# Retention and two MLPs on one core: the carried state as 128 rows by 64 columns, its products on 64x64 quarters of TensorE

## The chip, the cores and the metric

The kernel runs on one core of a Trainium2 chip. The time is device microseconds of one execution; 576.1 us is the median of three runs. Profiles hold one execution, with times from the start of its span.

## The reference

A retention layer (attention without softmax, computed block by block with a carried state) feeds two MLPs. The shapes are B = 2, H = 8 heads, S = 768 positions, D = 64 per head; the MLPs take 1536 tokens of width 512 to width 2048 and back, and every weight arrives as 64-bit floats.

```python
for b in range(nb):                        # blocks of positions
    intra = einsum('bhic,bhjc->bhij', qb, kb) * Dmask
    intra = einsum('bhij,bhjd->bhid', intra, vb)
    inter = einsum('bhid,bhde->bhie', qb * lam_pow, kv_state)
    out[:, :, sl] = intra + inter
    kv_state = lam_block * kv_state + einsum('bhsd,bhse->bhde', kb_dec, vb)
x = out.transpose(0, 2, 1, 3).reshape(B * S, H * D)
h = maximum(x @ w_in, 0.0);  x = h * h @ w_out          # first MLP
h = x @ w2_in;  return maximum(0.01 * h, h) @ w2_out     # second MLP
```

## The kernel before

**Units.** The retention works in 12 units: 2 batches times 6 blocks (c = 0 to 5) of 128 positions. The 8 heads are 4 head pairs p, and par = 0 or 1 is the head within its pair. A head's 64 columns lie on 64 partitions, so a pair fills 128. For one unit, TensorE transposes k and q (L294), multiplies the two to scores (L311, one PSUM bank for each par), forms the new state's addend from the decayed keys kd and v (L335), and forms the output (L360 and L362) as the sum of two products in one PSUM bank: the carried state times the scaled queries qS (only where c > 0, so in 10 of the 12 units), and v times the masked scores Pm.

**The state.** `st` is two tiles, used in turn, of 128 rows by 4 pairs by 128 columns. Each pair's 128x128 block is zero except for its two 64x64 diagonal blocks. The zeros are written once by POOL (L321). An update is done for each par by itself: POOL multiplies the old block by the decay (L342, `tmp`), and VectorE adds the PSUM addend (L347, or copies it where c = 0, L349).

**Array shapes.** The profile writes the part of TensorE that a matmul uses as rows*columns: 128*128 for transposes and the MLPs, 64*128 for scores, 128*64 for L335, L360 and L362 (two of these side by side cover the array). A float32 matmul is two instructions on the array; the MLPs' fp32r matmuls are one.

**Evacuation.** `split` copies the output bank to xhi on ScalarE (L68) and writes the rest to xlo on VectorE (L69). x is stored with head pairs as its four chunks of 128 rows; the first MLP contracts over these chunks.

**Order.** TensorE and the DMA queue of SyncE (SP) follow the program as written. In iteration i of the loop over units TensorE does the transposes of unit i + 2, the state addend of unit i, the output of unit i and the scores of unit i + 2. The order on VectorE, ScalarE and POOL is set by the scheduler when the program is built. All loads are issued by SP in one order: k, q, v of coming units, and in iterations 1 and 9 a chunk of the first MLP's weights (`fetch`, tile `raw`, 1 MB).

**Weights.** A fetched chunk is converted on the chip to two fp32r parts by `converting`: ScalarE takes the absolute value (L114) and a copy (L135), VectorE does six steps over 128x1024 elements (L115, L116, L118, L121, L122, L125) and a last one (L137). One step is taken in each of the iterations 3 to 9, and the rest beside the MLPs' matmuls. In some stages VectorE also forms sums of weight blocks (L437 to L442) and sums of activations (L449 to L451, L491) for a product scheme with seven instead of eight block products (`second_pair`).

**PSUM.** All tiles come from one pool of 8 banks; a unit takes six of them (two for transposes, one for the state, one for the output, two for scores).

**The MLPs.** All their matmuls are at L503. The first MLP is worked in four stages of 512 hidden columns, then the second in the same way.

## Time and profile before

| | |
|---|---|
| median of 3 runs | 576.1 us (575.93 to 576.34) |
| the profiled execution | 576.42 us, of which the span is 574.5 us |
| TensorE matmul busy | 564.2 us (98%) |
| VectorE, ScalarE, POOL busy | 418.4, 305.0, 83.9 us |
| granted TensorE clock | full (1.00) over the whole span |
| HBM read, written | 52.43 MB, 27.80 MB |

The span is the time from the first to the last instruction; 1.9 us of the execution lie around it. Busy time counts an engine as busy while any of its instructions is under way. Matmuls overlap, so a TensorE shown as busy can still have lost time between two starts; where that matters, starts are compared with starts.

### The profile page before, as it was taken

What the parts mean: (1) busy time and instruction counts of PE and PEld (TensorE: products, weight loads), DVE (VectorE), ACT (ScalarE), POOL (GpSimd) and SP (SyncE); (2) the same over time, 40 slices, a digit from 0 to 9 for tenths busy, and PEclk for the clock granted to TensorE, in tenths of its full rate; (3) what the DMA queues carried; (4) which work ended last, traced back from release to release, by engine and by line L of the source; (5) the groups of instructions that cost most, each with busy time, mean ns of one, the idle gap of its engine ahead of it and who ended that gap; (6) DMA issues with size and microseconds to landing.
All of it is one profiled execution on the core that took longest, in us unless ns stands there. A gap on an engine that the chain in (4) does not pass through costs nothing.

```text
span 574.5 us, 8051 instructions
## 1 busy us (share of the span) xinstructions
PE 564.2 (98%) x3075; PEld 470.7 (82%) x3075; DVE 418.4 (73%) x589; ACT 305.0 (53%) x477; POOL 83.9 (15%) x101
## 2 busy tenths in 40 slices
PE   7989999999999999999999999999999999999997
PEld 6878888888788888888888888888888888888886
DVE  3879999999927599498478999929873996217222
ACT  2344598546757687758448374553562376225110
POOL 3426000000040105445000000000203011310000
PEclk9999999999999999999999999999999999999999
DMA  8997434665492649999713216341529523661432
GB/s 172 239 213 177 156 121 138 234 183 180 172 164 57 73 148 181 203 249 189 185 36 91 76 41 216 128 165 74 103 55 246 109 29 47 76 90 56 162 113 92
DMA packets 74071, 78.12 MB, mean 136 GB/s; under 512 B 40105, under 2 KB 46513, under 8 KB 74033
## 3 DMA queue, kind: packets, MB, share of 16 engines
q1 hardware_dynamic: 60448, 60.57, 34.6%
q0 software_dynamic: 13056, 16.78, 20.9%
q8 instruction: 24, 0.39, 0.3%
q10 hardware_dynamic: 528, 0.26, 0.2%
q14 instruction: 15, 0.11, 0.1%
HBM read 52.43 MB, written 27.80 MB: 140 GB/s over the span
## 4 chain that ended last, share of the span: by engine, by line
PE 74%; DVE 15%; DMA 6%; issue 3%; SPq 1%; ACT 1%; POOL 0%; DVEq 0%; POOLq 0%; ACTq 0%
PE ps L503 72%; DMA raw<-in_moe_w_in 2%; DVE rb L122 2%; DMA raw<-in_moe_w_out 2%; DVE hb L125 2%; DVE hb L118 2%; SPq L65 1%; DVE rb L121 1%; DVE hb L115 1%; DVE Pm L316 1%; DMA k<-in_k 1%; DVE xlo L69 1%; DVE w1l L137 0%; DVE g1l L474 0%; DVE sw L442 0%
## 5 line engine op out<-in xcount | busy, mean ns | idle before, releaser
L503 PE MATMUL ps<-xhi,w1h 128*128 128x512 f32 x288 | 112.1, 389 | 0.0
L503 PE MATMUL ps<-xlo,w1h 128*128 128x512 f32 x288 | 112.0, 389 | 0.0
L503 PE MATMUL ps<-xhi,w1l 128*128 128x512 f32 x288 | 112.0, 389 | 0.0
L613 POOL DMA_DIRECT2D spill<-f x48 | 46.9, 1047 | 347.6 <-ACT f L609 347.5
L609 ACT COPY f<-ps 128x512 f32<-128x512 f32 x84 | 48.9, 586 | 74.1 <-PE ps L503 72.7
L503 PEld LDWEIGHTS ps<-xhi,w1h 128*128 128x128 f32 x288 | 54.1, 188 | 11.3 <-issue 0.2
L503 PEld LDWEIGHTS ps<-xlo,w1h 128*128 128x128 f32 x288 | 54.1, 188 | 11.3
L503 PEld LDWEIGHTS ps<-xhi,w1l 128*128 128x128 f32 x288 | 54.1, 188 | 11.2
L474 DVE TENSOR_TENSOR g0l<-f,g0h 128x512 fp32r<-128x512 f32 x52 | 35.1, 687 | 33.7 <-ACT f L470 22.1
L503 PE MATMUL ps<-w2l,g0h 128*128 128x512 f32 (+1 forms) x132 | 50.5, 383 | 0.0
L503 PE MATMUL ps<-w2h,g0l 128*128 128x512 f32 (+1 forms) x132 | 50.5, 383 | 0.0
L503 PE MATMUL ps<-w2h,g0h 128*128 128x512 f32 (+1 forms) x132 | 50.5, 383 | 0.0
L137 DVE TENSOR_TENSOR w2l<-hb,w2h 128x1024 fp32r<-128x1024 f32 x16 | 19.5, 1222 | 39.8 <-ACT w2h L135 39.8
L114 ACT ACTIVATE hb<-raw 128x1024 f32<-128x1024 f32 x32 | 36.8, 1150 | 19.2 <-DVE w2l L137 7.4
L503 PE MATMUL ps<-g0h,w2h 128*128 128x512 f32 x104 | 40.5, 389 | 0.0
L503 PE MATMUL ps<-g0l,w2h 128*128 128x512 f32 x104 | 40.5, 389 | 0.0
L503 PE MATMUL ps<-g0h,w2l 128*128 128x512 f32 x104 | 40.5, 389 | 0.0
L122 DVE SCALAR_TENSOR_TENSOR rb<-raw,rb 128x1024 f32<-128x1024 uint32 x32 | 39.1, 1221 | 0.4
L125 DVE TENSOR_TENSOR hb<-hb,rb 128x1024 f32<-128x1024 f32 x32 | 39.1, 1220 | 0.4
L118 DVE SCALAR_TENSOR_TENSOR hb<-raw,hb 128x1024 uint32<-128x1024 uint32 x32 | 39.1, 1220 | 0.3
L567 DVE TENSOR_TENSOR f<-ps,f 128x512 f32<-128x512 f32 x40 | 26.2, 684 | 9.9 <-PE ps L503 9.9
L714 DVE TENSOR_TENSOR f<-ps,f 128x512 f32<-128x512 f32 (+1 forms) x25 | 16.7, 669 | 22.9 <-PE ps L503 21.7
(141 smaller groups left out, 1139.4 us busy)
## 6 DMA issues: line engine op xcount, KB each, us to landing
raw<-in_moe_w_in SPq DMA_DIRECT2D x16, 1024.0 KB, 5.6
raw<-in_moe_w_out SPq DMA_DIRECT2D x16, 1024.0 KB, 5.0
spill<-f POOLq DMA_DIRECT2D x48, 256.0 KB, 4.8
spill<-f SPq DMA_DIRECT2D x24, 256.0 KB, 2.6
f<-spill SPq DMA_DIRECT2D x24, 256.0 KB, 2.9
k<-in_k SPq DMA_DIRECT2D x12, 256.0 KB, 4.9
q<-in_q SPq DMA_DIRECT2D x12, 256.0 KB, 5.1
v<-in_v SPq DMA_DIRECT2D x12, 256.0 KB, 4.8
```

The lines of the kernel that those rows point to most:

```text
L65: return nc.sync.dma_start(dst, src)
L114: nc.scalar.activation(hf, w_hi.bitcast(F32), AF.Abs)
L118: yield ve.scalar_tensor_tensor(out=hb, in0=w_hi, scalar=0xC0000000, in1=hb, op0=ALU.bitwise_and, op1=ALU.bitwise_or)
L122: yield ve.scalar_tensor_tensor(out=rf, in0=w_lo, scalar=2.0 ** -52, in1=rf, op0=ALU.mult, op1=ALU.mult)
L125: yield ve.tensor_tensor(out=hf, in0=hf, in1=rf, op=ALU.add)
L137: yield ve.tensor_tensor(out=lo, in0=hf, in1=hi, op=ALU.subtract)
L474: nc.vector.tensor_tensor(out=glo, in0=r, in1=ghi, op=ALU.subtract)
L503: nc.tensor.matmul(ps, a, b, start=start and n == 0, stop=stop and n == len(ops) - 1, skip_group_check=again)
L567: ve.tensor_tensor(out=out, in0=ps[h, where], in1=other, op=ALU.add)
L609: nc.scalar.copy(f, src)
L613: nc.gpsimd.dma_start(dst, f, accum_op=ALU.add)
L714: nc.vector.tensor_tensor(out=a, in0=ps, in1=a, op=ALU.add)
```

## The change

The state tiles become 128 rows by 4 pairs by 64 columns, without zeros: pair p's two heads stand below each other. The zeroing is gone, and an update is one POOL and one VectorE instruction over 128 rows in place of two over 64. In `output` each state product takes 64 rows and 64 columns of the array (64*64 in place of 128*64), and it can be any of the four quarters: for even pairs head par goes from rows half par to columns half par, for odd pairs to the other half. The eight state products of a unit now stand together, ahead of the eight of L362. The output takes two banks, one for even and one for odd pairs, so that `split` runs twice on half the elements. In x the two heads of an odd pair have changed places; the rows of the first MLP's first weight matrix are therefore fetched with the halves of odd chunks exchanged, by three DMAs in place of one (eight fetches, `raw` with l = 0 and n = 0).

```diff
+    half = [slice(e * D, (e + 1) * D) for e in range(2)]
...
-            dma(r.rearrange("p (k f) -> p k f", k=k), source(*key))
+            dst, src = r.rearrange("p (k f) -> p k f", k=k), source(*key)
+            if key[0] or key[2]:
+                dma(dst, src)
+            else:
+                dma(dst[:, 0:k:2], src[:, 0:k:2])
+                for a, b in ((half[0], half[1]), (half[1], half[0])):
+                    dma(dst[a, 1:k:2], src[b, 1:k:2])
...
-            st.append(att.tile([P, NP, P], F32, name=f"st{e}"))
-            nc.gpsimd.memset(st[e], 0.0)
+            st.append(att.tile([P, NP, D], F32, name=f"st{e}"))
...
-                for par in range(2):
-                    r = slice(par * D, (par + 1) * D)
-                    nc.gpsimd.tensor_tensor(out=tmp[r], in0=old[r, :, r],
-                                            in1=LR[r, :, C - 1:C].to_broadcast([D, NP, D]), op=ALU.mult)
-            for par in range(2):
-                r = slice(par * D, (par + 1) * D)
-                if c:
-                    nc.vector.tensor_tensor(out=new[r, :, r], in0=ps[r], in1=tmp[r], op=ALU.add)
-                else:
-                    nc.vector.tensor_copy(new[r, :, r], ps[r])
+                nc.gpsimd.tensor_tensor(out=tmp, in0=old, in1=LR[:, :, C - 1:C].to_broadcast([P, NP, D]), op=ALU.mult)
+                nc.vector.tensor_tensor(out=new, in0=ps, in1=tmp, op=ALU.add)
+            else:
+                nc.vector.tensor_copy(new, ps)
...
-            ps = bank().rearrange("p (a s) -> p a s", a=NP)
-            for p in range(NP):
-
-                rows = [slice(par * D, (par + 1) * D) for par in range(2)]
-                if c:
-                    for r in rows:
-                        nc.tensor.matmul(ps[r, p, :], st[c % 2][:, p, r], qS[n][:, p, :], start=True, stop=False)
-                for par, r in enumerate(rows):
-                    nc.tensor.matmul(ps[r, p, :], vn[:, 2 * p + par, :], Pm[n][:, par, p, :], start=c == 0, stop=True)
+            ps = [bank()[:, 0:2 * C].rearrange("p (a s) -> p a s", a=2) for _ in range(2)]
+            heads = [(p, par) for p in range(NP) for par in range(2)]
+
+            def place(p, par):
+                return ps[p % 2][half[par ^ p % 2], p // 2, :]
+
+            if c:
+                for p, par in heads:
+                    nc.tensor.matmul(place(p, par), st[c % 2][half[par], p, :], qS[n][half[par], p, :],
+                                     start=p < 2, stop=False, skip_group_check=True)
+            for p, par in heads:
+                nc.tensor.matmul(place(p, par), vn[:, 2 * p + par, :], Pm[n][:, par, p, :],
+                                 start=c == 0, stop=True, skip_group_check=True)
...
-            split(xhi[t][:, :, o:o + C], xlo[t][:, :, o:o + C], ps)
+            for e in range(2):
+                split(xhi[t][:, e::2, o:o + C], xlo[t][:, e::2, o:o + C], ps[e])
```

The scheduler also places some instructions of VectorE and ScalarE elsewhere. On ScalarE the place is the first conversion step (tile `hb`, L114 before and L123 after the change), in iteration 3 of the unit loop; kT and qT are the evacuated transposes of unit 5. First before, then after:

```order
L298 COPY kT<-ps 128x512
L298 COPY qT<-ps 128x512
L68 CAST xhi_278<-ps 128x4x128
L114 ACTIVATE hb<-raw 128x1024
L298 COPY kT<-ps 128x512
L298 COPY qT<-ps 128x512
L68 CAST xhi_278<-ps 128x4x128
```

```order
L307 COPY kT<-ps 128x512
L307 COPY qT<-ps 128x512
L68 CAST xhi_276<-ps 128x2x128 x2
L307 COPY kT<-ps 128x512
L307 COPY qT<-ps 128x512
L123 ACTIVATE hb<-raw 128x1024
L68 CAST xhi_276<-ps 128x2x128 x2
```

The conversion step that needs `raw` stood ahead of the two copies of that iteration and now stands behind them.

On VectorE the same iteration has the second conversion step (L115, after the change L124); st is the state, qS the scaled queries of unit 5. First before, then after:

```order
L316 TENSOR_TENSOR Pm<-ps,DTr 128x512 x2
L115 TENSOR_SCALAR hb<-hb 128x1024
L347 TENSOR_TENSOR st_168<-ps,tmp 64x4x64
L304 TENSOR_TENSOR qS<-ps,LR 128x512
L347 TENSOR_TENSOR st_168<-ps,tmp 64x4x64
L69 TENSOR_TENSOR xlo_279<-ps,xhi_278 128x4x128
```

```order
L325 TENSOR_TENSOR Pm<-ps,DTr 128x512 x2
L349 TENSOR_TENSOR st_168<-ps,tmp 128x256
L313 TENSOR_TENSOR qS<-ps,LR 128x512
L124 TENSOR_SCALAR hb<-hb 128x1024
L69 TENSOR_TENSOR xlo_277<-ps,xhi_276 128x2x128 x2
```

The state and the scaled queries moved ahead of the conversion step.

The third place is on VectorE too, in the second stage of the first MLP, ahead of the fourth `g1l` that `activate_for_seven` writes by `split` (L69), which is the last input of a product of `second_pair`. First before, then after:

```order
L488 TENSOR_TENSOR g0l<-f,g0h 128x512
L125 TENSOR_TENSOR hb<-hb,rb 128x1024
L491 TENSOR_TENSOR f<-f 128x512
L437 TENSOR_TENSOR rb<-hb 128x256
L438 TENSOR_TENSOR rb<-hb 128x256
L439 TENSOR_TENSOR rb<-rb,hb 128x256
L440 TENSOR_TENSOR rb<-hb,rb 128x256
L69 TENSOR_TENSOR g1l<-f,g1h 128x512
```

```order
L495 TENSOR_TENSOR g0l<-f,g0h 128x512
L127 SCALAR_TENSOR_TENSOR hb<-raw,hb 128x1024
L498 TENSOR_TENSOR f<-f 128x512
L130 TENSOR_SCALAR rb<-hb 128x1024
L131 SCALAR_TENSOR_TENSOR rb<-raw,rb 128x1024
L69 TENSOR_TENSOR g1l<-f,g1h 128x512
L134 TENSOR_TENSOR hb<-hb,rb 128x1024
L456 TENSOR_TENSOR f<-f 128x512
```

One conversion step over 1024 elements (L125, after the change L134) and the four weight sums over 256 moved from ahead of this `g1l` to behind it.

## Rows read from the trace of the kernel before

**Rows 1.** Chain that ended last, 125 to 575 us: start, us, what.
```profile
148.04 0.60 DVE g0l L488
149.84 1.14 DVE rb L122
153.32 0.34 DVE rb L437
...
155.44 174.61 PE ps L503 x769
...
329.83 241.34 PE ps L503 x1076
```

**Rows 2.** Busy time by stretch, each engine: retention, stage one and start of two, rest.
```profile
20.00:63.95 43.95, 42.16 (x674) 37.63 (x672) 37.73 (x62) 18.09 (x30) 16.47 (x20) 1.00 0.94 221
63.95:155.40 91.45, 90.96 (x401) 75.00 (x400) 89.18 (x113) 64.45 (x95) 0.00 (x0) 1.00 0.48 161
155.40:571.20 415.80, 415.70 (x1844) 344.53 (x1844) 280.59 (x379) 216.07 (x342) 59.27 (x64) 1.00 0.53 120
```

**Rows 3.** Timeline of one unit: start, us, engine, instruction, count.
```profile
23.04 0.66 PE L294 MATMUL ps<-ident,k 128*128 128x128 f32 x4
23.29 1.28 DVE L316 TENSOR_TENSOR Pm<-ps,DTr 128x512 f32<-128x512 f32 x2
...
24.06 0.69 PE L335 MATMUL ps<-v,kd 128*64 128x64 f32 x16
...
24.57 0.39 PE L360 MATMUL ps<-qS,st 128*64 128x128 f32 x4
...
24.80 0.39 PE L362 MATMUL ps<-Pm,v 128*64 128x128 f32 x4
...
26.11 0.39 PE L362 MATMUL ps<-Pm,v 128*64 128x128 f32 x4
...
26.42 1.16 PE L311 MATMUL ps<-qT,kT 64*128 64x128 f32 x16
...
27.52 0.66 PE L294 MATMUL ps<-ident,k 128*128 128x128 f32 x4
```

**Rows 4.** Groups by form: busy us, mean ns, idle before.
```profile
L347 DVE TENSOR_TENSOR st<-ps,tmp 64x256 f32<-64x256 f32 x16 | 6.7, 418 | 0.5 <-PE ps L335 0.3
...
L437 DVE TENSOR_TENSOR rb<-hb 128x256 f32<-128x256 f32 x1 | 0.4, 418 | 0.0
```

**Rows 5.** Timeline around the first conversion step.
```profile
22.76 1.13 SPq L65 DMA_DIRECT2D raw<-in_moe_w_in  x1
...
24.59 1.47 SPq L65 DMA_DIRECT2D q<-in_q  x1
...
30.60 1.12 ACT L114 ACTIVATE hb<-raw 128x1024 f32<-128x1024 f32 x1 [3.47 <-DMA raw<-in_moe_w_in]
...
31.53 1.04 POOL L329 TENSOR_TENSOR kd<-k,kdec 128x512 f32<-128x512 f32 x1 [4.32 <-DMA k<-in_k]
...
32.73 0.71 PE L311 MATMUL ps<-qT,kT 64*128 64x128 f32 x8 [1.76 <-ACT qT L298]
```

**Rows 6.** Tile q, 0 to 70 us: its loads from issue to landing.
```profile
DMA to landing us min/median/max: 4.0/5.1/7.7
```

**Rows 7.** Timeline of TensorE, outputs of the last two units.
```profile
61.63 0.76 PE L360 MATMUL ps<-qS,st 128*64 128x128 f32 x3
62.07 0.32 PE L362 MATMUL ps<-Pm,v 128*64 128x128 f32 x1
62.22 0.27 PE L360 MATMUL ps<-qS,st 128*64 128x128 f32 x1
```

**Rows 8.** Timeline, second stage of the first MLP.
```profile
154.30 0.61 PE L503 MATMUL ps<-g1h,sw 128*128 128x512 f32 x2
...
154.70 0.69 DVE L69 TENSOR_TENSOR g1l<-f,g1h 128x512 fp32r<-128x512 f32 x1
...
155.44 0.50 PE L503 MATMUL ps<-g1l,sw 128*128 128x512 f32 x1 [0.53 <-DVE g1l L69]
```

## The prediction

> **What bounds the kernel now.** I read the chain that ended last from its end backwards. From 155.44 us on it is nothing but MLP matmuls, in two pieces of 174.61 and 241.34 us [rows 1]; after 155.4 us TensorE is busy 415.70 of 415.80 us [rows 2]. What happens there can't be hurried by this change, which leaves the MLP matmuls alone: the end of the kernel is the time at which TensorE comes to this stretch, plus a constant. Ahead of it there are two more. In the retention (20 to 63.95 us) TensorE is busy 42.16 of 43.95 us, and in the stretch from 63.95 to 155.4 us 90.96 of 91.45, while VectorE with 89.18 us has hardly any room either [rows 2]. So time can come from four places: shorter TensorE work in each unit, the lost 1.8 us of the retention, small losses between starts, and the wait in which the third stretch begins.
>
> The reader should see each of them. A unit's period is 27.52 - 23.04 = 4.48 us [rows 3]. The one large stall is at 32.73: the scores wait 1.76 us for the copy of q, and that copy stands on ScalarE behind a conversion step that has waited 3.47 us for its weights [rows 5]. At 62 us the fourth state instruction of the last unit comes late (below) [rows 7]. At 155.44 a matmul waits for VectorE's g1l: its start is 1.14 us after the one at 154.30, where 0.23 is the pace (174.61/769) [rows 1, 8].
>
> **TensorE in a unit.** The sixteen state instructions and sixteen of L362 start in groups of four; from the first L360 group to the last L362 group are 26.11 - 24.57 = 1.54 us for seven steps, 0.22 us a group [rows 3]. Four instructions are two matmuls, so two halves of the array work at once and a round (one instruction on each half) takes 0.11 us. The state products take 8 rounds, 0.88 us. On four quarters they would take 4, 0.44 us: -0.44 a unit.
>
> Against it stand changes of array shape. Now a unit has three: L362 to L311, L311 to L294, L294 to L335. Sixteen score instructions (two at a time) are 0.88 us, eight transposes one at a time 0.88, L335 at half the columns 0.44, L360 and L362 1.76: 3.96 of the 4.48 us. The remaining 0.52 is 0.175 for each change, and the rows have them where the shape changes: L362's last group to L311 takes 0.31 rather than 0.22, L311's sixteen 1.10 rather than 0.88 [rows 3]. L335 and L360 have one shape today; after the change there are two more changes, into 64*64 and out of it: +0.35. The unit without a state addend ahead of its output (c = 5 of the first batch) gets one. Together 9 x (-0.44 + 0.35) + (-0.44 + 0.175) = -1.0 us over the ten units with c > 0. No row shows 64*64. Its bounds: changes that cost nothing (they are free now between L335 and L360) give -4.4; two quarters at once give +3.3; one at a time +12. I take -1.0, because column halves and row halves (L311) each run side by side at full rate here, and the quarters only join the two.
>
> **The stall at 32 us.** By the new order the two copies of unit 5 stand ahead of the conversion step on ScalarE. Then its scores need no weights, and the 1.76 us are free. Next is data: TensorE would come to unit 6's transposes at 27.52 + 4.40 = 31.9 us, and to its q at 32.4. POOL's instruction that waited for that k started at 31.53 [rows 5]; q was issued at 24.59 and took at most 7.7 us, so it is there by 32.3 [rows 5, 6]. Both just arrive. Ahead of them in SP's queue the fetch is three issues for one of 1.13 us. Two more cost nothing if the transfers are the limit (the DMA share is 0.94 over this stretch [rows 2]) and 2.3 us if every issue takes 1.13, of which only what lies behind 31.9 and 32.4 counts. I take 0.1: -1.7 us; bounds -1.8 and 0. What is late next is the conversion itself, which stays at the landing of raw, 30.6. On VectorE behind it are xlo and the masks, first needed by the scores one unit later, over 3 us on. The other seven fetches have three issues as well; the second comes at the retention's end, the rest where TensorE is the bound, and I cost them nothing: 2.3 us at the second if that cover is gone.
>
> **VectorE, ScalarE, POOL.** Cost goes by columns, not rows: 64x256 and 128x256 both take 418 ns [rows 4]. In a row, 256 elements occupy VectorE for 0.34 us, 512 for 0.60, 1024 for 1.14 [rows 1]. An update saves 0.34, a split into two costs 2 x 0.34 - 0.60 = +0.08. From the conversion step at 31.75 to the g1l at 154.70 the order after has 8 such state instructions less (-2.7), 9 splits more (+0.7), the scaled queries moved ahead (-0.6), and the 1024-element step and four sums behind g1l instead of ahead (-2.5): -5.1 us.
> ScalarE's split adds less than one copy a unit (0 to 0.59 us); it is busy 18 of 44 us in the retention, POOL, with one of two updates gone, 16.5 [rows 2]: nothing on the path.
>
> **The small losses.** At 61.63 three L360 instructions start, then L362 at 62.07 and the fourth L360 only at 62.22, since the second state half is written later. L362 would have started 0.22 after 61.63. One update for both halves, ready earlier: -0.2 us, bounds -0.4 and 0.
>
> At 155 us TensorE arrives 2.9 us earlier (1.0 + 1.7 + 0.2), where it used to lose 1.14 - 0.23 = 0.9. VectorE's g1l then must be 3.8 us earlier than its end at 155.39 for no wait; it has 5.1 us less ahead of it. So -0.9 us, if the order is gone through as it stands; 0 or +0.3 if the moved steps return ahead of g1l.
>
> **PSUM.** A unit takes seven banks rather than six, so with eight the second score bank of one unit is the first of the unit before, free when VectorE has masked it. The mask at 23.29 is done with its first half at 23.93; the scores that would need its bank begin at 26.42 [rows 3]. 2.5 us of room: no cost.
>
> **Sum.** -1.0 - 1.7 - 0.2 - 0.9 = -3.8 us. The profiled execution took 576.42, which gives 572.6; it was 0.3 above the median, so against the median it is 572.3. I say 572.4.
>
> **Rivals.** (a) Two quarters at a time. The two instructions of one matmul are for the same quarter; if starts go strictly in program order, each matmul's second instruction holds up the next matmul, and a round is one matmul: 8 rounds, no gain, +3.3 for the shape changes. Against: at 62.07 an L362 instruction started ahead of an L360 instruction that stands before it and goes to the other half [rows 7]. 576.4 - 1.7 + 3.3 - 0.2 - 0.9 = 576.9, 576.6 against the median.
> The Trainium skill, "TensorE: Matmul & The Clock Gate", Part 3, says that matmuls start and end in program order, without reordering; that is this rival, and the start at 62.07 disagrees. The Trainium skill, "TensorEngine Tiling (Array Packing)", Restrictions and Gotchas, adds that different row tiles can't use one PSUM bank at the same time; here both heads of an even pair, from two row halves, write one bank (in different rows of it), which would also leave two at a time. No run here shows this.
> (b) Slower: quarters one at a time. Sixteen instructions at 0.11 are 1.76 us, 0.88 more, with the changes +1.23 a unit: +12, in all 576.4 + 12 - 2.8 = 585.6. It decides at this place alone: with -2.8 from the rest, the kernel is over 0.2% (1.15 us) slower once the state products with both changes take over 0.88 + 0.40 = 1.28 us. For it: no row has quarters; against: halves of both kinds run side by side.
> (c) The waits come back. k and q of unit 6 arrive 1.5 us late behind the three-part fetch, and g1l waits for VectorE as before (0.9 and 0.3 more): -3.8 + 2.7 = -1.1, 575.0 against the median.
> (d) Shape changes beside 128*64 cost nothing: TensorE gains 3.4 more, of which VectorE at 155 us lets through about half: 571 to 570.5.
>
> **How the numbers follow.** Forecast 0.57 (own range 571.2 to 573.8), (a) 0.13, (b) 0.06, (c) 0.15, (d) 0.09. Within 0.2% of 576.1 is 574.95 to 577.25, about what a measurement of this kernel can tell from no change. Faster: 0.57 + 0.09 + half of (c) = 0.73. Same: the other half of (c) and most of (a), 0.18. Slower: (b) and the rest of (a), 0.09. The range 570.8 to 576.9 leaves out (b), and parts of (d), (a) and the forecast, about 0.2.
>
> **What would show it.** Right: eight state instructions of a unit at 64*64 in two groups, 0.11 us from round to round with four starts in each, and two new gaps of some 0.2 us around them; units of 4.3 to 4.4 us; no wait of TensorE for the copy of q at 32 us; MLP matmuls from about 61.0 rather than 63.95; no wait for g1l near 152. Wrong: rounds of two or one; TensorE waiting for k, q or the mask; a stretch of MLP matmuls that has gaps where VectorE's moved steps are now needed.

## The result, and the profile after

| | before | after |
|---|---|---|
| median of 15 runs each on one chip | 576.34 us (575.57 to 580.11) | 581.9 us (577.39 to 585.53) |
| ratio | | 1.0086 (95%: 1.0065 to 1.0106) |
| the profiled execution | 576.42 us, span 574.5 | 577.39 us, span 575.6 |

Slower by 0.9%, where 572.4 was forecast, and outside the range. The profiled execution after is the fastest of its 15 runs. It has 1.0 us of the loss; the other 4.5 us up to the median must be looked for in another run (the first experiment).

The retention stage does what was said of it. The timeline of a unit in the kernel after, TensorE (start, time, line, shape, count), beside [rows 3]:

```profile
23.95 0.69 PE L343 MATMUL ps<-v,kd 128*64 128x64 f32 x16
24.56 0.67 PE L364 MATMUL ps<-qS,st 64*64 64x128 f32 x16
25.16 1.09 PE L367 MATMUL ps<-Pm,v 128*64 128x128 f32 x16
26.18 1.16 PE L320 MATMUL ps<-qT,kT 64*128 64x128 f32 x16
...
28.91 0.55 PE L364 MATMUL ps<-qS,st 64*64 64x128 f32 x11
```

L364 is the state product. Its sixteen instructions take 25.16 - 24.56 = 0.60 us to the next shape (forecast 0.44 and a change of 0.175), and L367's take 1.02 (0.88 and a change). A narrow window, 24.61 to 24.62 us, holds the first round alone:

```profile
24.56 0.34 PE L364 MATMUL ps<-qS,st 64*64 64x128 f32 x4
```

Four instructions have started by then, one for each quarter. The unit is 28.91 - 24.56 = 4.35 us long (forecast 4.39, before 4.48). So four quarters do work at once, and a change of shape costs about what the rows of before gave for it.

The data come later, though. TensorE and SP around 22 to 35 us, beside [rows 5]:

```profile
32.51 0.63 PE L303 MATMUL ps<-ident,k 128*128 128x128 f32 x4 [0.82 <-DMA k<-in_k]
33.61 0.63 PE L303 MATMUL ps<-ident,q 128*128 128x128 f32 x4 [0.47 <-DMA q<-in_q]
35.06 0.45 PE L343 MATMUL ps<-v,kd 128*64 128x64 f32 x8 [0.82 <-DMA v<-in_v]
```

```profile
22.35 2.49 SPq L65 DMA_DIRECT2D raw<-in_moe_w_in  x3
24.93 1.38 SPq L65 DMA_DIRECT2D k<-in_k  x1
```

The wait for the copy of q (1.76 us) is gone, as forecast; three waits for loads behind the three-part fetch, 2.11 us together, stand in its place. The first MLP matmul starts at 62.65 us, 1.3 ahead of before; forecast was 61.0.

From there on even that is lost. The windows of the kernel after, cut as in [rows 2] (length, then busy time of TensorE, weight loads, VectorE, ScalarE, POOL; granted clock, DMA share, GB/s):

```profile
20.00:63.95 43.95, 41.84 (x681) 34.65 (x680) 34.66 (x63) 19.70 (x43) 11.88 (x13) 1.00 1.01 220
63.95:155.40 91.45, 90.54 (x400) 74.66 (x399) 88.47 (x110) 64.14 (x96) 0.00 (x0) 1.00 0.48 151
155.40:571.20 415.80, 414.12 (x1836) 343.03 (x1835) 281.86 (x383) 215.48 (x341) 58.92 (x64) 1.00 0.53 122
```

The third stretch, busy 415.70 us before, now has 1.7 us without a matmul. From the first to the last start of an MLP matmul it takes 571.91 - 62.65 = 509.26 us after, 506.92 before: 2.34 lost, 1.30 gained, 1.04 slower. Two waits make it up (TensorE, then ScalarE at the second):

```profile
154.52 0.50 PE L510 MATMUL ps<-g1l,sw 128*128 128x512 f32 x1 [0.91 <-DVE g1l L69]
...
224.95 0.50 PE L510 MATMUL ps<-g1h,sw 128*128 128x512 f32 x1 [1.68 <-ACT f L616]
```

```profile
224.31 1.08 ACT L616 COPY f<-ps 128x512 f32<-128x512 f32 x2 [3.13 <-DMA partial0P<-f]
```

The first is the wait of [rows 8], still there (0.91 for 0.53). The second is new: ScalarE must copy a bank out, it has to wait for an `f` buffer, and the transfer that frees it (partial0P) takes 7.0 us to land, 5.0 before, beside a weight fetch issued 0.4 us behind it (before, 1.4 us ahead of it). That fetch is a chunk of the second weight matrix, which is still one transfer.

VectorE's stream shows why the first wait stayed:

```profile
63.25 0.69 DVE L124 TENSOR_SCALAR hb<-hb 128x1024 f32<-128x1024 f32 x1 [1.16 <-ACT hb L123]
...
117.28 0.69 DVE L124 TENSOR_SCALAR hb<-hb 128x1024 f32<-128x1024 f32 x1 [0.98 <-ACT hb L123]
...
151.31 0.69 DVE L498 TENSOR_TENSOR f<-f 128x512 f32<-128x512 f32 x1
151.91 0.69 DVE L130 TENSOR_SCALAR rb<-hb 128x1024 uint32<-128x1024 uint32 x1
152.64 1.23 DVE L131 SCALAR_TENSOR_TENSOR rb<-raw,rb 128x1024 f32<-128x1024 uint32 x1
153.78 0.69 DVE L69 TENSOR_TENSOR g1l<-f,g1h 128x512 fp32r<-128x512 f32 x1
```

L124 is the first VectorE step of a conversion; it waits for ScalarE's L123, which waits for `raw`. At 62 and 116 us VectorE stands still for weights that have not landed, 2.1 us between 60 and 155 us (0.6 before). The chunk at 62 us came in three parts; the one at 116 us is of the second matrix, in one transfer that took 6.5 us to land (4.9 before):

```profile
116.12 1.13 ACT L123 ACTIVATE hb<-raw 128x1024 f32<-128x1024 f32 x1 [2.74 <-DMA raw<-in_moe_w_out]
```

So g1l starts at 153.78, 0.9 earlier than before, where 3.8 were needed. The windows from the first VectorE step of the first conversion to this g1l, before and after, say how (the third busy time is VectorE's):

```profile
31.75:154.70 122.95, 121.94 (x896) 102.86 (x896) 119.76 (x162) 77.86 (x118) 13.24 (x15) 1.00 0.58 173
```

```profile
32.66:153.78 121.12, 119.66 (x880) 98.80 (x879) 114.31 (x157) 76.75 (x124) 8.96 (x9) 1.00 0.61 169
```

VectorE has 5.45 us less to do, as the prediction counted (5.1). But it stands still for 6.81 us in place of 3.19 and begins 0.91 later: -5.45 + 3.62 + 0.91 = -0.92.

### The profile page after: what moved, and what is told of

Read it like the earlier page. It is cut to its first block, busy times and chain, and to the rows that moved or that the text cites. A ratio compares the mean times of both kernels' runs of the same rounds, so it can differ in the third digit from the quotient of the medians.

```text
span 575.6 us, 8079 instructions
## 1 busy us (share of the span) xinstructions
PE 564.0 (98%) x3075; PEld 467.8 (81%) x3075; DVE 415.2 (72%) x591; ACT 305.6 (53%) x489; POOL 77.1 (13%) x91
## 4 chain that ended last, share of the span: by engine, by line
PE 74%; DVE 10%; issue 6%; DMA 6%; ACT 3%; POOL 0%; SPq 0%; DVEq 0%; ACTq 0%; POOLq 0%
PE ps L510 67%; DMA raw<-in_moe_w_out 2%; DVE rb L131 2%; DVE hb L127 2%; PE ps L303 2%; PE ps L367 2%; PE ps L320 1%; DMA v<-in_v 1%; DVE hb L134 1%; DMA partial0P<-f 1%; DMA raw<-in_moe_w_in 1%; DVE hb L124 1%; ACT hb L123 1%; DVE w2l L146 1%; DVE rb L130 1%
## 5 line engine op out<-in xcount | busy, mean ns | idle before, releaser
L616 ACT COPY f<-ps 128x512 f32<-128x512 f32 x84 | 48.4, 587 | 72.9 <-PE ps L510 69.6
L123 ACT ACTIVATE hb<-raw 128x1024 f32<-128x1024 f32 x32 | 36.8, 1149 | 23.8 <-DMA raw<-in_moe_w_in 9.0
L134 DVE TENSOR_TENSOR hb<-hb,rb 128x1024 f32<-128x1024 f32 x32 | 39.1, 1222 | 0.4
```

The lines of the kernel that those rows point to most:

```text
L123: nc.scalar.activation(hf, w_hi.bitcast(F32), AF.Abs)
L134: yield ve.tensor_tensor(out=hf, in0=hf, in1=rf, op=ALU.add)
L616: nc.scalar.copy(f, src)
```

## The experiments

Theory at first: the three-part fetch is what costs (F). Rivals: the waits, or the quarter products, pull the clock down (C); the new order on VectorE and ScalarE costs (S). Later, theory R: up to 157 us the end is set by VectorE, and VectorE by the landing of `raw`. All columns behind the ratio are of one profiled execution, whose time stands first and can lie far from the median (after, e3, e16). "Start" is the first MLP matmul, "raw" VectorE's waits at the first conversion step from 60 to 155 us, "150s" TensorE's waits from 145 to 165 us, "220s" its wait at 222 to 232 us, "low" the time at a granted clock of 0.50 after 20 us. Ratios are to the kernel before on the same chip (576.0 to 576.65).

An edit of the fetches also moves the order in which the scheduler places work on VectorE and ScalarE, so most pairs of runs differ in both. Two pairs do not: e17 has the order of the kernel before, and e4 that of e2, on TensorE, VectorE, ScalarE and POOL, from the first instruction to the last.

| run | median | ratio (95%) | profiled | start | raw | 150s | 220s | low |
|---|---|---|---|---|---|---|---|---|
| before | 576.3 |  | 576.42 | 63.95 | 0.6 | 0.5 | 0 | 0 |
| after | 581.90 | 1.0065 to 1.0106 | 577.39 | 62.65 | 2.1 | 0.9 | 1.7 | 0 |
| e1 after again | 580.51 | 1.0038 to 1.0085 | 580.87 | 62.39 | 4.5 | 2.9 | 1.8 | 3.4 |
| e2 one transfer | 579.46 | 1.0026 to 1.0078 | 581.99 | 61.36 | 4.8 | 5.3 | 0 | 6.8 |
| e3 before, three parts | 582.38 | 1.0081 to 1.0124 | 579.36 | 63.67 | 3.6 | 1.3 | 1.7 | 0 |
| e4 no exchange | 578.96 | 1.0028 to 1.0062 | 579.01 | 64.95 | 2.8 | 1.9 | 0 | 0 |
| e5 early fetch | 580.89 | 1.0057 to 1.0096 | 577.81 | 62.73 | 2.2 | 1.2 | 1.4 | 0 |
| e6 ahead | 584.03 | 1.0116 to 1.0157 | 584.59 | 69.41 | 2.2 | 1.1 | 1.6 | 6.8 |
| e7 filler at 153 us | 578.81 | 1.0027 to 1.0068 | 578.48 | 62.76 | 3.6 | 0.2 | 1.3 | 0 |
| e8 before, ahead | 577.16 | 1.0009 to 1.0027 | 576.75 | 63.74 | 2.4 | 0.9 | 0 | 0 |
| e9 after, no fetches | 576.80 | 1.0000 to 1.0024 | 578.59 | 67.23 | 0.3 | 0 | 0 | 6.8 |
| e10 before, no fetches | 579.53 | 1.0036 to 1.0064 | 579.53 | 67.89 | 0.3 | 0 | 0 | 0 |
| e11 gain burnt | 580.61 | 1.0043 to 1.0088 | 582.58 | 65.47 | 2.8 | 1.1 | 2.1 | 3.4 |
| e12 rows put right in x | 581.58 | 1.0050 to 1.0093 | 584.28 | 66.03 | 1.8 | 2.6 | 0 | 3.4 |
| e13 reorder | 582.68 | 1.0107 to 1.0133 | 582.29 | 62.25 | 3.1 | 3.2 | 1.6 | 6.8 |
| e14 before, reorder | 576.57 | 1.0001 to 1.0019 | 576.29 | 62.61 | 1.1 | 1.6 | 0 | 0 |
| e15 both reorders | 584.27 | 1.0104 to 1.0165 |  |  |  |  |  |  |
| e16 one transfer, reorder | 578.73 | 1.0028 to 1.0068 | 576.00 | 61.47 | 1.1 | 2.5 | 0 | 0 |
| e17 before, three of 128 | 581.05 | 1.0054 to 1.0112 | 581.22 | 64.05 | 2.8 | 3.2 | 0 | 3.4 |
| e18 before, two of 64 | 578.71 | 1.0028 to 1.0055 | 578.15 | 65.46 | 1.0 | 0 | 0.7 | 0 |

**e1.** The changed kernel word for word.

> The changed kernel once more, for a second trace of it. Theory F (the fetch in three parts delays the loads behind it and puts the weights in the way of other transfers): about 578 to 583 us, waits for k, q and v near 32 us again, and further waits that end in a DMA. Rival C (TensorE's granted clock falls in the changed retention, by the new quarter products or by the waits): the same time, but with a stretch at 0.5 that this trace shows away from the first 20 us.

Slower again, and this time the profiled execution (580.87) is near the median. VectorE and TensorE in it:

```profile
63.98 0.69 DVE L124 TENSOR_SCALAR hb<-hb 128x1024 f32<-128x1024 f32 x1 [2.15 <-ACT hb L123]
...
119.29 0.69 DVE L124 TENSOR_SCALAR hb<-hb 128x1024 f32<-128x1024 f32 x1 [2.39 <-ACT hb L123]
```

```profile
154.70 0.50 PE L510 MATMUL ps<-g1h,sw 128*128 128x512 f32 x1 [1.58 <-ACT g1h L68]
156.51 0.80 PE L510 MATMUL ps<-g1l,sw 128*128 128x512 f32 x1 [1.31 <-DVE g1l L69]
```

and its windows:

```profile
152.73:156.03 3.30, 0.90 (x3) 0.19 (x1) 3.27 (x5) 1.94 (x4) 0.00 (x0) 1.00 0.00 0
156.03:159.44 3.41, 2.92 (x7) 2.35 (x8) 3.41 (x6) 2.37 (x5) 0.76 (x1) 0.50 0.60 190
159.44:226.20 66.76, 66.76 (x296) 55.29 (x295) 45.80 (x64) 45.98 (x73) 12.40 (x15) 1.00 0.57 122
```

The same program waits 2.4 us longer for `raw` than in the first profile, TensorE stands still 2 us longer, and behind this the granted clock is 0.50 (the 1.2 GHz level) for 3.41 us: 7 matmuls where 15 fit, 1.8 us. With that the loss of this execution against the profile of before, 580.87 - 576.42 = 4.45 us, is accounted for: -1.56 (start), +2.4 (150s), +1.8 (clock), +1.8 (220s), together 4.4. Over the 24 runs of the changed kernel, the 8 with a mean clock of 0.997 or more took 577.0 to 579.7 us, the 16 with 0.994 or less 580.4 to 585.5. In the kernel before, run beside the experiments, 28 of 111 runs had a mean clock under 0.996 and no loss (median 576.29, the others 576.14). A low clock in the start-up, as in the profile of e3 (0.50 from 12.3 to 19.1 us), costs next to nothing: its MLPs started at 63.67.

**e2, e3, e4.** e2 is the changed kernel with one transfer for each chunk, e3 the kernel before with the fetch in three parts. In both, x and the rows of the first weight matrix then stand in different orders: the work is the same, the sums are not the layer's. e4 is the changed kernel with odd pairs placed like even ones (two quarters) and one transfer. The edit of e2:

```diff
-            if key[0] or key[2]:
-                dma(dst, src)
-            else:
-                dma(dst[:, 0:k:2], src[:, 0:k:2])
-                for a, b in ((half[0], half[1]), (half[1], half[0])):
-                    dma(dst[a, 1:k:2], src[b, 1:k:2])
+            dma(dst, src)
```

> The changed kernel with each chunk fetched by one DMA again; the rows of odd chunks of the first weight matrix are then not exchanged, so the product uses them in the old order. Theory F: 572 to 574 us, retention's end near 61 us, k of unit 6 at about 31.5, little spread between runs. Rival C, and a rival S (the new order on VectorE and ScalarE): 578 us or more with the same spread.

> The kernel before with the three-part fetch alone; the rows of odd chunks of the first weight matrix are exchanged although x is not. Theory F: 578 to 582 us with the spread of the changed kernel. Rivals C and S: 576 to 577 us, as before.

> The changed kernel with one DMA for a chunk and with odd pairs placed like even ones: the state products use two of the four quarters, and x keeps its order. Theory F: 3 to 4 us more than with four quarters, that is 576 to 577. Rival C by quarter products: near the changed kernel, 578 to 582. Rival C by waits: as theory F.

e3, just above theory F's range, shows that the fetch, with the order that the scheduler makes for it, makes the kernel before 1.0% slower. Its list of waits of TensorE from 145 to 232 us has the wait of the 220s, which the profiles with pieces of 64 partitions in every fetch of the first matrix have and no other:

```profile
PE ps L511 <- ACT f L617: 1.7, 1, 1.7
PE ps L511 <- DVE g1l L69: 1.3, 1, 1.3
```

e2 starts the MLPs at 61.36, near the forecast 61.0, so the three parts cost 1.3 us there. But F is not all (it had 572 to 574): e2 is still 0.5% slower, and loses it in the 150s:

```profile
PE ps L505 <- ACT g1h L68: 2.5, 1, 2.5
PE ps L505 <- DVE g0l L490: 1.9, 1, 1.9
PE ps L505 <- DVE g1l L69: 0.9, 1, 0.9
```

```profile
157.53:164.35 6.82, 6.08 (x14) 4.78 (x15) 5.30 (x9) 4.11 (x8) 1.89 (x2) 0.50 0.61 165
```

Again a low clock behind it (14 matmuls in 6.82 us, 3.6 lost). Its VectorE waits 3.0 us for one chunk, issued at 117.4 and converted from 126.6:

```profile
127.77 0.69 DVE L119 TENSOR_SCALAR hb<-hb 128x1024 f32<-128x1024 f32 x1 [3.00 <-ACT hb L118]
```

The order differs as well: in e2 and e4 the conversion step over 1024 elements and the four sums stand ahead of the g1l at 154 us again, as in the kernel before.

e4 missed theory F's 576 to 577. It shows something else. With two quarters TensorE is slower in each unit, and the first MLP matmul comes 3.59 us later than in e2 (64.95 for 61.36; F had 3 to 4 us for it). But with the same order of instructions on every engine VectorE reaches its g1l at the same time, in e2 and then in e4:

```profile
157.53 0.68 DVE L69 TENSOR_TENSOR g1l<-f,g1h 128x512 fp32r<-128x512 f32 x1
```

```profile
157.41 0.68 DVE L69 TENSOR_TENSOR g1l<-f,g1h 128x512 fp32r<-128x512 f32 x1
```

and the median is no later (578.96 for 579.46). In these executions the 3.6 us that the four quarters win for TensorE are gone at this g1l. They need not be: the three fastest of e2's twelve runs took 575.3 to 575.9 us, the fastest of e4's seven 577.6.

**e5 to e8.** e5 fetches the second chunk at unit 7 (`if i in (1, 7)`), e6 at unit 6 and with a conversion step in each of the last two units (`3 <= i <= 11`); e8 is e6's edit in the kernel before. e7 puts nine products nobody reads ahead of the ones that wait at 153 us:

```diff
+        if s == 1:
+            fill(9)
         for p in both:
             keep(product(p, "C", "S1", "T1"), kept(p, 1, 1), False)
```

> The changed kernel with one number edited: the second weight chunk is fetched two units earlier in the retention loop (at unit 7 instead of 9), when its raw buffer has long been free. Theory R (the stretch up to 157 us is set by VectorE, and VectorE's place there by when the raw words arrive: it idles from about 62 to 63.3 or 64 us for the second chunk): that idle time goes, VectorE comes 1.2 to 2.1 us earlier, the wait for g1l at 153 us shrinks to under 0.5 us, the granted clock does not fall behind it, and the median is 575.5 to 577.5. Rival C (the clock falls because of the quarter products in the retention stage, or for some other reason than the waits): the waits get shorter but the median stays at 580 or more with a mean clock of 0.99. Rival T (TensorE has to wait for something else just behind it, so that an earlier VectorE brings nothing): the median stays at 579 to 581 with new waits between 153 and 160 us.

> The changed kernel with the second weight chunk fetched at unit 6 instead of 9 and one step of conversion put into each of the last two units of the retention stage as well. Theory R (VectorE's place at 153 us is what counts, and it has idle time in the retention stage): two steps (about 1.9 us) leave the MLP stretch on top of what the early fetch brings, no wait of over 0.4 us at 149 to 158 us, median 574.5 to 576.5, that is as fast as the kernel before or faster. Rival C (clock from the products themselves): 580. Rival T: the wait is handed on, 578 to 580.

> The changed kernel with nine extra products of 128x512 (2.0 us) in TensorE's order just ahead of the products that wait at 153 us, into a bank that nobody reads. Theory R with the clock behind the waits (the wait at 153 us is real, and the low granted clock at 156 us follows from TensorE's standing still there): the nine products fill the wait and are nearly free, the granted clock stays at 1.0 behind it, the runs draw together, and the median falls from 580.5 to 577.5 to 579. Rival C (the clock falls for another reason): the clock still falls at 156 us and the nine products cost up to 2 us: 581 to 583.

> The kernel before with the second chunk fetched at unit 6 and one conversion step in each of the last two retention units, nothing else. Theory R: the kernel before has a wait of 0.9 us for g1l at 154 us and VectorE is busy from 64 us on; steps put into the retention stage take that wait away and it gains 0.5 to 1.2 us: 575.0 to 575.6. Rival T: no change within 0.3 us, 575.9 to 576.4. If the steps are in the way of the retention stage itself (they would end a unit later), it is slower by 0.5 to 2 us.

e5 is a miss: the wait at 62 us went, as R said, but VectorE gave the lead back (waits for `raw` at 114 and 139 us), TensorE waited 1.2 us in the 150s, and nothing was gained. e6 and e8 are misses too: in e6 TensorE waited 3.0 us for a k that was loaded behind the early fetch, and was clocked at 0.50 behind that (start 69.41); e8 lost 0.9 us, what it expected if the steps are in the way. e7 agrees with R and the clock behind the wait: nine products, 2.0 us, ran inside the wait (0.2 left), and the clock stayed at 1.0 there. Its median lies 1.7 us below that of e1, on another chip, and the ranges of the two ratios overlap; that the added work costs nothing can be said, that it gains can't.

**e9, e10.** No weight fetches but the first; every conversion reads that chunk again.

```diff
+            if only:
+                fetched.append((key, only[0]))
+                return
             r = raw.tile([P, 4 * CW], I64, tag="raw", name="raw")
+            only.append(r)
```

> The changed kernel without its weight fetches: only the first chunk is fetched (in three parts, as before), and every later conversion reads that chunk's raw words again, so all weights are the first chunk's. Conversions, products, spills and everything else stay. Theory R (the gain of the retention stage is real, and is lost because VectorE waits for raw words on the way to 153 us): the MLP stretch takes 507 us or less from a start at 61 to 62.5 us, no wait of over 0.5 us at 149 to 160 us, granted clock 1.0; 571 to 574 us, and 2 to 3 us below the kernel before with the same left out. Rival O (the order of VectorE's work is at fault, not the data): the wait at 153 us stays over 1 us, the granted clock falls behind it in many of the runs, and the time is 577 to 580, at or above the twin.

> The twin: the kernel before, fetching the first chunk alone and converting it again and again. In the kernel before VectorE waits for raw words hardly at all (0.3 us between 64 and 155 us), so by theory R little is gained: 574.5 to 576, which leaves it 2 to 3 us above the changed kernel's twin. Rival O: 575 to 576, and the changed kernel's twin is no faster.

The MLP stretch of e9, and one row of e10:

```profile
67.23:155.00 87.77, 87.77 (x388) 72.70 (x388) 84.48 (x111) 61.15 (x91) 0.00 (x0) 1.00 0.10 37
155.00:225.00 70.00, 70.00 (x311) 57.97 (x310) 48.91 (x66) 50.68 (x81) 13.81 (x16) 1.00 0.44 75
...
```

```profile
67.89:155.00 87.11, 87.11 (x385) 72.14 (x385) 84.18 (x108) 61.40 (x90) 0.00 (x0) 1.00 0.10 37
```

Without fetches TensorE does not miss a beat from the first to the last MLP matmul, 506.1 us in both, and the changed kernel is 2.7 us the faster of the two. Theory R had the difference and missed the rest: both start late (67.2 and 67.9, not 61 to 62.5), and both times lie above their ranges. With words always there the scheduler puts more conversion steps into the retention, in e10 with waits of TensorE for VectorE's state. So this pair changes the order as well as the data. The profiled execution of e9 (578.59) lies above its median; it has three waits for k, q and v around 33 to 36 us, 3.4 us together, and a low clock beside them:

```profile
35.06:41.89 6.83, 5.85 (x64) 5.05 (x64) 5.95 (x11) 1.79 (x5) 1.04 (x1) 0.50 1.09 215
```

That the difference comes so near the 2.9 us forecast for the retention is luck in part: the forecast took 1.7 of them from the wait for the copy of q, which is 0.6 us in e10, and had k, q and v in time, which they are not in e9.

**e11, e12.** e11 burns the gain: nine products nobody reads, ahead of the first MLP product. e12 has one transfer and puts the rows right in x, by two copies of 64 partitions for odd pairs.

> The changed kernel with nine extra products of 128x512 (2.04 us at full clock) ahead of the first MLP product, into a bank that nobody reads: they burn the gain of the retention stage on TensorE. The scheduler orders VectorE's work anew behind them. Theory R with the clock behind the waits (TensorE's earlier arrival is not what the time hangs on, and standing still at 153 us costs the clock as well): the wait at 153 us gets shorter by about as much as was burnt (under 0.4 us left), the granted clock stays at 1.0 in most runs, and the median is 577.5 to 579.5, below the changed kernel's 580.5 to 581.9 in spite of the added work. Rival C (the clock falls for another reason): the burnt time is added, 582 to 584.

> The changed kernel with every chunk fetched in one transfer and the rows put right on the other side: the output of odd head pairs is copied and split in two pieces of 64 partitions, each written to the other half of x (two more ScalarE and two more VectorE instructions per unit), so that the weights keep their order. By theory R the retention stage still ends near 61 to 62 us, VectorE waits less for raw words than the changed kernel (under 3 us between 60 and 155 us in place of 4.1), and the median is 576.5 to 579. If the extra instructions of a unit are in the way (VectorE late for the masks), the MLP starts at 63 to 64 us and the time is 578 to 580. If the order of VectorE's work counts and not the fetch, it stays at 579 to 581, as with one transfer and the weights left in their order.

In e11 TensorE came 2.8 us later to the MLPs than in the changed kernel, and the median is that of e1 (580.61 for 580.51). It was not below it, as I had expected: 1.1 us of waits were left in the 150s where under 0.4 was expected, and a wait of 2.1 us in the 220s had a low clock behind it. But the later start cost nothing, as in e4. e12 is a miss: it starts at 66.03 (waits for copies of q and for the state, 4.2 us), ends above all its ranges and tells nothing on the fetch.

**e13 to e16.** TensorE's order at 153 us, so that g1l has 2.7 us more (e13, in the kernel before e14, with one transfer e16); e15 also moves S4 behind S2 at 223 us.

```diff
-        for p in both:
-            keep(product(p, "C", "S1", "T1"), kept(p, 1, 1), False)
-            yield True
-        late_split("T3", "T1", lambda h: (1, 2 * h))
         for p in both:
             keep(product(p, "A", "A12", "B21", False), kept(p, 0, 0), False)
             yield True
         late_split("T4", "B21", lambda h: (0, 2 * h + 1))
+        if s == 1:
+            yield from c_products()
```

> The changed kernel with one edit in TensorE's order: in the second stage (around 153 us) the four groups that read g1 for the first time (C, S1 with T1) stand behind the four that read g0 (A, A12 with B21) and no longer ahead of them, so that the late g1l has 2.7 us more. VectorE's order up to there is the same. Theory W (what the changed kernel loses at 149 to 158 us is the standing still of TensorE there, and the low clock behind it): no gap over 0.5 us between 149 and 160 us, no low clock behind it, the wait of about 2 us at 223 us stays; median 577.5 to 579 (after 580.5 to 581.9). Rival V (VectorE's stream is late and sets all that follows): the gap moves to a later product of the same stage (157 to 165 us) with the same length, median 580 to 582.

> The kernel before with the same edit in TensorE's order. Theory W: its wait of 0.9 us at 154 us goes, 575.2 to 575.8. Rival V: no change, 576.0 to 576.6.

> The changed kernel with that edit, and in the third stage (around 223 us) the groups that add to bank C (S4 with B22) put behind the two that follow them (S2 with T2), so that ScalarE's copy of C, which stands still for an f buffer whose transfer to memory is late, has 2.7 us more. Theory W (both waits are all that is left): both gaps gone, MLP stretch 506.5 to 507.5 us from a start at 62.5 us, median 574.5 to 576.5, level with the kernel before or below. Rival V: the second gap stays or moves, 578 to 581.

> The changed kernel with every chunk fetched in one transfer (the rows of the first weight matrix are then not exchanged to match x) and the first of the two edits of order. With one transfer the start was at 61.4 us and the loss lay in gaps of 6 us together at 149 to 158 us, and none at 223 us. Theory W: gaps of 3 us or less are covered, two thirds of the loss goes: 575 to 577 (579.5 without the edit). Rival V: 579 to 580.

Rival V held in e13 (a little above its range) and e14; e15 came out above both ranges, e16 between them. In e13 the wait was handed on and grew (TensorE, VectorE and ScalarE):

```profile
155.55 0.80 PE L510 MATMUL ps<-g0h,w2h 128*128 128x512 f32 x1 [3.25 <-ACT f L616]
```

```profile
151.86 0.68 DVE L498 TENSOR_TENSOR f<-f 128x512 f32<-128x512 f32 x1
```

```profile
152.58 0.62 ACT L68 CAST g1h<-f 128x512 fp32r<-128x512 f32 x1 [1.35 <-DVE f L498]
...
154.93 1.05 ACT L616 COPY f<-ps 128x512 f32<-128x512 f32 x2
```

A12 adds to the bank that ScalarE must first copy out (L616), and this copy stands on ScalarE behind g1h, which waits for VectorE's L498. So this product, too, waits for VectorE. The profile of e15 is of an execution of 1459.5 us and is not read; its other runs give no gain.

**e17, e18.** The kernel before with three transfers of the changed kernel's sizes over all 128 partitions (e17), and with one transfer for each half of the partitions (e18).

```diff
                 dma(dst[:, 0:k:2], src[:, 0:k:2])
-                for a, b in ((half[0], half[1]), (half[1], half[0])):
-                    dma(dst[a, 1:k:2], src[b, 1:k:2])
+                for j in range(1, k, 2):
+                    dma(dst[:, j:j + 1], src[:, j:j + 1])
```

> The kernel before, whose chunks of the first weight matrix are fetched in three transfers of the same sizes as in the changed kernel (512, 256 and 256 KB), but each over all 128 partitions. Theory H (transfers into 64 partitions are what is slow: the chunk's 2 KB packets take 126 to 130 ns in the three-part form and 90 to 100 ns in one piece): the packets take 90 to 105 ns, no wait of 2 us at 224 us, 576.0 to 578, well below the 582.4 of the three parts with pieces of 64 partitions. Theory N (three issues in place of one, and the order that the scheduler makes for them, are what is slow): as with the pieces of 64, 580 to 583, and the gap of 2 us at 224 us.

> The kernel before, whose chunks of the first weight matrix are fetched in two transfers of 512 KB, one for each half of the partitions. Theory H: all packets go to 64 partitions at a time, so as slow as the three-part form or slower, packets of 120 ns and more, 580 to 584. Theory N: one issue more than before only, 576.5 to 579.

The window from 58 to 60 us, in which the second chunk comes in, of the kernel before, e3 and e17 (the last number is GB/s):

```profile
58.00:60.00 2.00, 2.00 (x44) 1.71 (x39) 1.94 (x5) 0.59 (x1) 0.99 (x2) 1.00 1.09 419
```

```profile
58.00:60.00 2.00, 2.00 (x42) 1.88 (x42) 1.94 (x5) 0.59 (x1) 1.24 (x2) 1.00 1.00 217
```

```profile
58.00:60.00 2.00, 2.00 (x42) 1.71 (x40) 1.94 (x5) 0.58 (x1) 0.90 (x2) 1.00 0.99 319
```

With pieces of 64 partitions the DMA engines are as busy (1.00) and bring half as much as one transfer, and two thirds of what three transfers over all partitions bring. The Trainium skill, "SBUF — State Buffer", Door 1: The DMA port swizzle, says that partitions 0 to 63, or 64 to 127, reach only half of SBUF's sixteen DMA ports; 217 GB/s beside 319 and 419 agrees in direction. The window shows the contrast at its largest: from 56 to 62 us the means are 358 (before), 268 (e3) and 315 (e17). So theory H is right that these transfers are slower.

It is wrong on the time: e17 loses 0.8% all the same, and e3's 1.0% can't be told from it. e18 ends in theory N's range. And e17 settles more than that. VectorE, ScalarE, POOL and TensorE have the instructions of the kernel before, in the same order, from the first to the last; only SP has sixteen issues more. Up to the same g1l VectorE is as long busy as before (119.81 for 119.76 us), but it stands still 2.9 us more (6.10 for 3.19), and g1l comes at 157.77, 3.1 us later:

```profile
31.86:157.77 125.91, 123.34 (x914) 103.54 (x909) 119.81 (x162) 77.22 (x118) 12.91 (x15) 1.00 0.57 167
```

```profile
157.09 0.50 PE L511 MATMUL ps<-g1h,sw 128*128 128x512 f32 x1 [2.31 <-ACT g1h L68]
158.51 0.50 PE L511 MATMUL ps<-g1l,sw 128*128 128x512 f32 x1 [0.92 <-DVE g1l L69]
```

No change of order on these engines has a part in this; the weights that land later do it. Of the 2.9 us, 2.2 are waits for `raw` after 60 us.

The wait of the 220s goes with pieces of 64 partitions, and e17 has none. But the fetch that runs beside the store there is never such a piece. In every run that has the wait, the store takes 6.6 to 7.0 us to land and a whole chunk of the second matrix is issued 0.4 us behind it; in the runs that fetch and do not wait there, 4.9 to 5.2 us, with that chunk 1.4 us ahead. So what costs there is the order of the issues, and that has moved in each of the runs with pieces and in no other.

## Why the prediction was wrong

**Held.** The quarters (0.60 us for the state products, unit 4.35 us): rivals (a) and (b) are refuted, though both heads of an even pair write one bank from two row halves. The shape changes (0.175 each): rival (d) too. The wait for the copy of q at 32 us is gone. With one transfer the MLPs start at 61.36 and 61.47 (e2, e16) for the forecast 61.0. The count of VectorE's work held as well: 5.1 us less forecast, 5.45 measured.

One reading that spoke against rival (a) was too strong. At 62.07 an L362 instruction does start ahead of the second instruction of an L360 product. But the first instruction of that product had started just before:

```profile
62.06 0.32 PE L360 MATMUL ps<-qS,st 128*64 128x128 f32 x1
```

So the products began in their order there, and only the two instructions of neighbouring ones are interleaved. Against the rival that was enough.

**Failed, a size: the fetch at 32 us.** "I take 0.1: -1.7 us; bounds -1.8 and 0." The three issues took 2.49 us, k, q and v came late by 2.11 us together, and the start is 1.3 us later than with one transfer: -0.4 in place of -1.7, near the other bound.

**Failed, the step that decides: "the other seven fetches have three issues as well ... and I cost them nothing".** They ran beside a stretch that I had read as TensorE's. It is VectorE's as much, and VectorE's pace is that of the loop in which a raw buffer is freed, fetched, landed and converted. In the kernel before this loop just closes (VectorE waits 0.6 us for it between 60 and 155 us). After, it waits 2.1 us in the first profile and 4.5 in that of e1, for whole chunks of the second matrix as well as for split ones. Three transfers for one, with the order on the four engines held, make g1l 3.1 us late and the kernel before 0.8% slower (e17). With pieces of 64 partitions it is 1.0% (e3), as much as the whole change, and the wait in the 220s comes on top, 1.7 us.

**Failed with it: "VectorE's g1l ... has 5.1 us less ahead of it".** The count stands; the place does not follow from it, since VectorE does not run through. It stood still 3.62 us more than before in one profile and 6.26 in the other, so that g1l came 0.9 us earlier in the first and 1.1 later in the second (155.78):

```profile
32.18:155.78 123.60, 120.67 (x894) 99.57 (x890) 114.15 (x158) 76.12 (x124) 8.08 (x9) 1.00 0.59 166
```

The -0.9 for that wait was +0.4 in the profiled run and +2.4 in e1.

**Failed, the frame: "the end of the kernel is the time at which TensorE comes to this stretch, plus a constant".** TensorE may come 3.6 us later at no cost to the median, with the same order on every engine (e4 beside e2). A TensorE that is early stands still in the 150s, and then the clock can take 1.8 to 3.6 us more. Rival (c), "the waits come back", was the right mechanism at the wrong price: it had no term for the clock, none for the 220s, and g1l at 0.9 + 0.3.

**Open.** e2, e4 and e16 show 0.45 to 0.5% of loss without the three parts. Waits for `raw` and the order of VectorE and ScalarE both differ from before there, with a conversion step and four sums back ahead of g1l, and no run parts the two. Nor is it shown why the landing of the same transfers differs so much from run to run, or why some waits of TensorE have a low clock behind them and others none.

No version beat the kernel before. Of those that compute the layer, e14, which is the kernel before with one edit, came nearest to it (within 0.2%).

## What to carry to other kernels

When an engine looks 98% bound, ask what its neighbour at 97% waits for: if the neighbour lives off a loop of two buffers, a gain upstream turns into a wait at the point where the two meet. Less work ahead of an instruction does not make it earlier by as much: add up busy time and idle time apart. Cost a transfer that is split or moved in every place where it runs, not only where it is first seen. And look for a run whose order of instructions is that of its twin: one such pair (e17 beside before, e4 beside e2) says more than several in which the scheduler has moved things as well.

## What was not expected of the hardware

A wait of TensorE can cost more than its length: behind waits of 2.9 us (e1), 3.2 (e17) and 5.3 (e2) in the 150s the granted clock was 0.50, the 1.2 GHz level, for 3.41 us in the first two and for 6.82 in e2. It is not certain: behind 3.2 us in e13 it was 0.50 for 6.83 us, and e16 waited 2.5 us and stayed at 1.00. The Trainium skill, "DMA: Bandwidth & Descriptors", Rules for kernel authors, advises one transfer over 128 partitions in place of two over its halves. e18, where that is the whole edit, is 0.42% slower, so the run agrees; its profile has the loss in a start 1.5 us later and in the 220s, and the scheduler's order has changed there too.
